# Retention attention, a capacity-routed mixture of experts and a gated MLP on one core: expert outputs stored from ScalarE's queue, five staging buffers, and new numbers in the planner

## The chip, the core and the metric

The kernel runs on one core of a Trainium2 chip. The metric is device time in microseconds for one execution; runs of an unchanged kernel here lay between 903.23 and 906.43 us. Everything is float32 outside; most products are made of three float32r matmuls (high part by high part, low by high, high by low).

## The reference

```python
# 1: retention attention, q, k, v: (4, 8, 576, 64)
scores = (q @ k.T) / sqrt(64);  out = (scores * decay(gamma_h, i - j, causal)) @ v
x = out.transpose(0, 2, 1, 3).reshape(2304, 512)
# 2: 8 experts, each token to one expert, cap = 288 tokens each
logits = x @ w_gate
for idx in argsort(-logits.flatten()):        # greedy, best logit first
    tok, e = idx // 8, idx % 8
    if assigned[tok] < 0 and counts[e] < cap: assigned[tok] = e; counts[e] += 1
for e in range(8): out[assigned == e] = relu(x[assigned == e] @ w1[e]) @ w2[e]   # 512 -> 1024 -> 512
# 3: 512 -> 2048 -> 512
h = x @ w_in;  return (h * tanh(softplus(h))) @ w_out
```

## The kernel before

There are three stages. **Attention** walks over 18 tiles of 128 tokens, computes the gate's logits and stores x in DRAM. **Experts**: the greedy assignment is rebuilt as a search. In each of 8 rounds the expert that fills first is found by VectorE (DVE) and TensorE (PE) in turn: six threshold steps, each a comparison `G` on DVE, 18 small matmuls `pF`, a test `sat`, one matmul `pD`. The round then gives the expert's number `eid`, the marks of its tokens, and through `pI` the list `idx` of its 288 tokens. GpSimd (POOL) gathers these rows of x into `xg` by three indirect DMAs; PE transposes them (`mmx`), ScalarE (ACT) rounds them to `xh`, DVE makes the rest `xl`. The expert's weights come in 8 units of 512 KB: SyncE (SP) reads `eid` into a register (line 532) and issues each load into a staging buffer `st` (3 of them); ACT rounds it to `whi` (line 562), POOL, late in the stage DVE too, makes `wlo` (line 565), after which the staging buffer is free. `whi` and `wlo` lie in a ring of 12. Per expert PE runs 96 matmuls `mma` (first layer; after every 12, ACT makes `hh` and DVE `hl`, which frees the PSUM bank) and 96 `mmb` (second layer, four outputs `y`). ACT copies each `y` out of PSUM (line 787) and SP stores it to `y_scratch` (line 650). There are 32 such stores of 144 KB.

In between, the weights of stage 3, which arrive as float64, are narrowed to float32 in 32 pieces: SP loads `std`, ACT makes `words`, DVE shifts (line 725) and joins into `dw` (line 728), ACT makes `dt`, POOL multiplies, SP stores `dw` to DRAM. **The last stage** reads y in 6 tiles of 384 tokens and the narrowed weights in 16 units (the same `st`, `whi`, `wlo`), and alternates per step 12 matmuls `mmc` and 9 matmuls `po`, with a gate of ACT, DVE and POOL operations between them.

From the experts on, the order on every engine is fixed when the program is built, by a planner inside the kernel. Every piece of work is a Python generator that yields the engine, an estimated duration, the events that it waits for and a priority; the planner keeps a clock per engine and emits the instruction that could start first. Each engine then runs its list strictly in order, SP's list of DMA issues too: an instruction whose input is late holds back everything behind it on that engine. An estimate that is short of the truth so puts an instruction too early in its list.

Of the kernel before, what the change touches and what calls it, by code (L numbers as in the profile page):

```python
# [7 lines left out]
F32 = mybir.dt.float32  # L8
# [9 lines left out]
P = 128  # L18
# [15 lines left out]
REST = 64.0  # L34
NRING = 12
YB = 4
# [7 lines left out]
GATHER = 7500  # L44
# [86 lines left out]
class Kernel:  # L131
# [188 lines left out]
    def routing_setup(self):  # L320
# [5 lines left out]
        self.onef = pr.tile([P, NT], F32, name="onef")  # L326
        nc.gpsimd.memset(self.onef, 1.0)
        self.digit = pr.tile([64, 6, P], BF16, name="digit")
# [45 lines left out]
    def route(self):  # L374
# [8 lines left out]
        for i in range(E):  # L383
# [4 lines left out]
            if i == E - 1:  # L388
# [3 lines left out]
                self.spawn(self.weights_of(junk, at))  # L392
                rest = rw.tile([P, NT], F32, name="rest")
                v.tensor_scalar(rest, self.dead, -1.0, 1.0, op0=ALU.mult, op1=ALU.add)
                v.tensor_tensor_scan(scan[:, 0], self.onef, rest, 0.0, op0=ALU.mult, op1=ALU.add)
# [14 lines left out]
            for s in range(6):  # L410
                m = WIDTHS[s]
                if s or i:
# [34 lines left out]
                    at = yield PE, 80 + 15 * m, [at], 0  # L447
# [8 lines left out]
            at = yield DVE, 2100, [at], 0  # L456
# [11 lines left out]
            over = self.at("over").rearrange("p (j t) -> p j t", j=2)  # L468
            v.tensor_tensor(over[:, 0], key, theta.to_broadcast([P, NT]), op=ALU.is_gt)
            v.tensor_tensor(over[:, 1], key, theta.to_broadcast([P, NT]), op=ALU.is_equal)  # L470
            of = over
# [14 lines left out]
            if i:  # L486
                self.widen(i, ohe)
                self.spawn(self.weights_of(junk, at))
                choice = yield from self.choose(i, at)
            at = yield DVE, 1600, [marked, at], 0  # L490
            pose = rw.tile([P, NT], F32, name="pose")
            v.scalar_tensor_tensor(pose, scan[:, 1], pP[:, 1:2], eq, op0=ALU.add, op1=ALU.mult)
            v.scalar_tensor_tensor(pos, scan[:, 0], pP[:, 0:1], gt, op0=ALU.add, op1=ALU.mult)
            fin = self.at("fin")
            v.scalar_tensor_tensor(fin, pose, CAP + 0.5, eq, op0=ALU.is_lt, op1=ALU.mult)
            if i == 0:
                self.spawn(self.weights_of(junk, at))
            v.tensor_tensor(self.dead, self.dead, gt, op=ALU.add)
            v.tensor_tensor(self.dead, self.dead, fin, op=ALU.add)
            v.tensor_tensor(pose, pose, fin, op=ALU.mult)  # L500
            v.tensor_tensor(pos, pos, pose, op=ALU.add)
# [19 lines left out]
    def weights_of(self, junk, at):  # L521
# [9 lines left out]
        at = yield SP, 1000, [at], 0  # L531
# [116 lines left out]
    def store(self, dst, src, at, done=None):  # L648
        at = yield SP, DMA_ISSUE, [at], 1
        self.nc.sync.dma_start(dst, src)  # L650
        if done is not None:
            done.append(self.arrival(100000, at))
# [10 lines left out]
    def y_place(self):  # L663

        n = self.made - YB
        return Event(0) if n < 0 else self.stored[n] if n < len(self.stored) else None

# [34 lines left out]
    def narrow(self):  # L702
# [4 lines left out]
        def at(k, n):  # L707
            return [lambda: done[k].get(n)] if n >= 0 else []

        def load():  # L710
            for n in range(32):
# [3 lines left out]
                now = yield SP, DMA_ISSUE, [Event(0), *at("read", n - 3)], self.narrow_priority  # L715
# [4 lines left out]
        def piece(n, st, now, dst):  # L720
# [5 lines left out]
            now = yield DVE, 680, [now, *at("store", n - 3)], self.narrow_priority  # L726
            out = self.conv.tile([P, 512], U32, name="dw", bufs=3)
# [10 lines left out]
            now = yield SP, DMA_ISSUE, [now], self.narrow_priority  # L738
# [27 lines left out]
    def experts(self):  # L766
        nc, a = self.nc, self.a
        for i in range(E):
# [14 lines left out]
            def result(i, d, bank, at):  # L783
                at = yield ACT, 410, [at, self.y_place], 0
# [295 lines left out]
```

## Time and profile before

| | |
|---|---|
| median of 3 runs | 904.78 us (903.23 to 906.43) |
| profiled execution, its own time | 900.87 us |
| its span, first to last instruction | 899.1 us |
| busy: PE, DVE, POOL, ACT | 810.1, 682.9, 484.0, 407.8 us |
| mean granted TensorE clock | 0.937 of full speed |

The profile comes from one execution, which was 0.4% quicker than the median; sums on its rows belong beside 900.87. Shares of the whole span hide that the stages have different limits, so the rows further down are cut by stage: attention to about 100 us, the first routing to 144, experts from 144 to about 460, the last stage from there.

### The profile page before, as it was taken

What the parts mean: (1) busy time and instruction counts of PE and PEld (TensorE: products, weight loads), DVE (VectorE), ACT (ScalarE), POOL (GpSimd) and SP (SyncE); (2) the same over time, 40 slices, a digit from 0 to 9 for tenths busy, and PEclk for the clock granted to TensorE, in tenths of its full rate; (3) what the DMA queues carried; (4) which work ended last, traced back from release to release, by engine and by line L of the source; (5) the groups of instructions that cost most, each with busy time, mean ns of one, the idle gap of its engine ahead of it and who ended that gap; (6) DMA issues with size and microseconds to landing.
All of it is one profiled execution on the core that took longest, in us unless ns stands there. A gap on an engine that the chain in (4) does not pass through costs nothing.

```text
span 899.1 us, 15492 instructions
## 1 busy us (share of the span) xinstructions
PE 810.1 (90%) x5833; PEld 726.6 (81%) x5833; DVE 682.9 (76%) x1104; ACT 407.8 (45%) x736; POOL 484.0 (54%) x406
## 2 busy tenths in 40 slices
PE   7999767969796979776999899997999999999997
PEld 5888636868786969676998789986899899999995
DVE  4344574748584768583778999998899899899894
ACT  1221214434443444434666655544655645645543
POOL 4533015756564566553424776755755655655644
PEclk9999888969897879896999999998999999999999
DMA  9982146777777777779976300200100100100000
GB/s 341 357 268 76 71 87 221 198 149 194 188 200 182 197 174 207 186 161 266 336 240 200 117 19 1 71 1 1 53 19 1 59 13 1 62 10 0 36 1 36
DMA packets 66331, 112.37 MB, mean 125 GB/s; under 512 B 10192, under 2 KB 38224, under 8 KB 66256
## 3 DMA queue, kind: packets, MB, share of 16 engines
q1 hardware_dynamic: 63280, 101.94, 39.8%
q0 software_dynamic: 2976, 9.44, 3.5%
q8 instruction: 46, 0.75, 0.4%
q14 instruction: 29, 0.24, 0.1%
HBM read 88.81 MB, written 22.55 MB: 124 GB/s over the span
## 4 chain that ended last, share of the span: by engine, by line
PE 54%; DVE 20%; DMA 18%; POOL 3%; issue 2%; ACT 1%; SPq 1%; POOLq 0%; DVEq 0%; ACTq 0%
PE mmc L959 15%; PE po L1020 15%; PE mma L753 9%; DVE q L989 8%; DMA st<-w 7%; DMA xg<-x_scratch,idx 5%; PE mmb L753 4%; DVE n L984 3%; DMA std<-w_in 3%; PE pA L200 2%; PE pT L228 2%; PE pT L231 2%; PE pL L241 2%; PE pF L450 1%; DVE n L994 1%
## 5 line engine op out<-in xcount | busy, mean ns | idle before, releaser
L989 DVE RECIPROCAL q<-q 128x384 f32<-128x384 f32 x96 | 244.3, 2545 | 10.6 <-ACT q L987 9.1
L565 POOL TENSOR_TENSOR wlo<-st,whi 128x1024 fp32r<-128x1024 f32 x53 | 125.8, 2384 | 99.3 <-ACT whi L562 92.7
L991 POOL TENSOR_TENSOR n<-n,q 128x384 f32<-128x384 f32 x96 | 102.0, 1062 | 99.3 <-DVE q L989 94.9
L1001 POOL TENSOR_TENSOR gl<-n,gh 128x384 fp32r<-128x384 f32 x96 | 109.0, 1135 | 55.6 <-ACT gh L999 55.3
L959 PE MATMUL mmc<-yh,whi 128*128 128x384 f32 x384 | 130.8, 341 | 8.0 <-DVE n L994 7.9
L959 PE MATMUL mmc<-yl,whi 128*128 128x384 f32 x384 | 130.5, 340 | 5.0 <-POOL yl L919 4.7
L959 PE MATMUL mmc<-yh,wlo 128*128 128x384 f32 x384 | 130.3, 339 | 0.0
L562 ACT CAST whi<-st 128x1024 fp32r<-128x1024 f32 x80 | 83.4, 1047 | 83.2 <-DMA st<-w 79.0
L1020 PE MATMUL po<-whi,gl 128*128 128x512 f32 x288 | 114.6, 398 | 0.0
L1020 PE MATMUL po<-wlo,gh 128*128 128x512 f32 x288 | 114.4, 397 | 0.0
L1020 PE MATMUL po<-whi,gh 128*128 128x512 f32 x288 | 112.8, 392 | 0.0
L984 DVE SCALAR_TENSOR_TENSOR n<-s 128x384 f32<-128x384 f32 x96 | 104.1, 1086 | 3.2 <-ACT s L977 2.5
L977 ACT ACTIVATE s<-mmc 128x384 f32<-128x384 f32 x96 | 47.1, 491 | 117.4 <-PE mmc L959 105.0
L753 PE MATMUL mma<-xh,whi 128*128 128x288 f32 x256 | 84.4, 330 | 6.8 <-ACT xh L624 4.4
L959 PEld LDWEIGHTS mmc<-yh,whi 128*128 128x128 f32 x384 | 72.7, 189 | 14.9 <-DVE n L994 9.1
L753 PE MATMUL mma<-xh,wlo 128*128 128x288 f32 x256 | 83.4, 326 | 0.0
L753 PE MATMUL mma<-xl,whi 128*128 128x288 f32 x256 | 83.1, 325 | 0.0
L959 PEld LDWEIGHTS mmc<-yl,whi 128*128 128x128 f32 x384 | 72.8, 189 | 10.1 <-POOL yl L919 5.3
L753 PE MATMUL mmb<-hl,whi 128*128 128x288 f32 x256 | 78.4, 306 | 0.0
L753 PE MATMUL mmb<-hh,wlo 128*128 128x288 f32 x256 | 77.7, 304 | 0.0
L753 PE MATMUL mmb<-hh,whi 128*128 128x288 f32 x256 | 77.7, 304 | 0.0
L736 POOL TENSOR_TENSOR dw<-dw,dt 128x512 f32<-128x512 f32 x32 | 48.5, 1516 | 48.0 <-ACT dt L732 45.3
(149 smaller groups left out, 1643.6 us busy)
## 6 DMA issues: line engine op xcount, KB each, us to landing
st<-w SPq DMA_DIRECT2D x64, 512.0 KB, 6.1
qk<-qk SPq DMA_DIRECT2D x18, 512.0 KB, 4.8
kv<-kv SPq DMA_DIRECT2D x18, 512.0 KB, 5.2
std<-w_in SPq DMA_DIRECT2D x16, 512.0 KB, 8.2
std<-w_out SPq DMA_DIRECT2D x16, 512.0 KB, 5.7
x_scratch<-xs SPq DMA_DIRECT2D x18, 256.0 KB, 2.8
y_scratch<-y SPq DMA_DIRECT2D x32, 144.0 KB, 6.0
yt<-y_scratch SPq DMA_DIRECT2D x22, 192.0 KB, 2.7
```

Source lines behind the costliest of these rows:

```text
L200: nc.tensor.matmul(pA[i][:, hp, :], QK[t][sl, 1, hp, :], QK[t][sl, 0, hp, :], start=True, stop=True)
L562: self.nc.scalar.copy(dst[0], st)
L565: (self.nc.vector if lo.engine == DVE else self.nc.gpsimd).tensor_tensor(dst[1], st, dst[0].bitcast(F32), op=ALU.subtract)
L736: nc.gpsimd.tensor_tensor(out, out, t, op=ALU.mult)
L753: self.nc.tensor.matmul(bank[1][:, :CAP], al if h == 2 else ah, bl if h == 1 else bh, start=(first and j == h == 0), stop=(last and j == n ...
L959: self.nc.tensor.matmul(bank[1][:, :TILE], (wl if h == 2 else wh)[:, c, cs], x[c][h == 1], start=(c == h == 0), stop=(c == HP - 1 and h == 2))
L977: nc.scalar.activation(s, p, AF.Sigmoid)
L984: v.scalar_tensor_tensor(u, s, 2.0, s, op0=ALU.subtract, op1=ALU.mult)
L989: v.reciprocal(q, q)
L991: nc.gpsimd.tensor_tensor(u, u, q, op=ALU.mult)
L1001: nc.gpsimd.tensor_tensor(gl, u, gh.bitcast(F32), op=ALU.subtract)
L1020: nc.tensor.matmul(po[j], (gl if h == 2 else gh)[:, js], (wl if h == 1 else wh)[:, f % 2], start=(f == h == 0), stop=(f == DFF // P - 1 an ...
```

## The change

- `result` no longer hands y to SP: ACT issues the store itself, directly behind its own copy. The planner counts the store as done 6,000 ns later (`STORED`).
- Staging buffers: `STAGES = 5` in place of 3. `dw` has 2 buffers in place of 3.
- Estimates: a gather takes 10,000 ns in place of 7,500, a product's matmul 150 in place of 132, `pF` 90 + 17m in place of 80 + 15m, the copy of y 480 in place of 410, two DVE stretches of the routing less.
- SP's instructions are planned 4,000 ns behind what they wait for (`APART`): the list store, the store of `dw`, the reload of `std`, the read of `eid` from the second expert on.
- Routing on DVE: the choice of tokens above and at the threshold takes one mask and two fused operations in place of two comparisons and two fused operations; one running sum over 36 columns replaces two over 18; after it, `dead` is updated once from `pos` in place of twice. Per round 13 operations become 10.

```diff
+STORED = 6000
+APART = 4000
+STAGES = 5
...
-GATHER = 7500
+GATHER = 10000
...
-            for j in range(2):
-                v.scalar_tensor_tensor(of[:, j], top, best[:, 0:1], over[:, j], op0=ALU.is_equal, op1=ALU.mult)
...
-            for j in range(2):
-                v.tensor_tensor_scan(scan[:, j], self.onef, of[:, j], 0.0, op0=ALU.mult, op1=ALU.add)
+            chosen = rw.tile([P, NT], F32, name="chosen")
+            v.tensor_scalar(chosen, top, best[:, 0:1], None, op0=ALU.is_equal)
+            v.scalar_tensor_tensor(gt, key, theta[:, 0:1], chosen, op0=ALU.is_gt, op1=ALU.mult)
+            v.scalar_tensor_tensor(eq, key, theta[:, 0:1], chosen, op0=ALU.is_equal, op1=ALU.mult)
+            v.tensor_tensor_scan(scan.rearrange("p j t -> p (j t)"), self.onef, self.at("over"), 0.0, op0=ALU.mult, op1=ALU.add)
...
-            v.tensor_tensor(self.dead, self.dead, gt, op=ALU.add)
-            v.tensor_tensor(self.dead, self.dead, fin, op=ALU.add)
...
+            v.scalar_tensor_tensor(self.dead, pos, 0.5, self.dead, op0=ALU.is_gt, op1=ALU.add)
...
-        at = yield SP, 1000, [at], 0
+        at = yield SP, 1000, [at if i == 0 else Event(at.t + APART)], 0
...
-        place = [lambda: self.staged.get(n - 3)] if n >= 3 else []
+        place = [lambda: self.staged.get(n - STAGES)] if n >= STAGES else []
...
-            now = yield DVE, 680, [now, *at("store", n - 3)], self.narrow_priority
-            out = self.conv.tile([P, 512], U32, name="dw", bufs=3)
+            now = yield DVE, 680, [now, *at("store", n - 2)], self.narrow_priority
+            out = self.conv.tile([P, 512], U32, name="dw", bufs=2)
...
-            now = yield SP, DMA_ISSUE, [now], self.narrow_priority
+            now = yield SP, DMA_ISSUE, [Event(now.t + APART)], self.narrow_priority
...
-                at = yield PE, 132, [lambda: (term() or (0, None))[1], *([] if bank else [self.bank])], 2
+                at = yield PE, 150, [lambda: (term() or (0, None))[1], *([] if bank else [self.bank])], 2
...
-                at = yield ACT, 410, [at, self.y_place], 0
+                at = yield ACT, 480, [at, self.y_place], 0
...
-                yield from self.store(a["y"][:, d, i * CAP:(i + 1) * CAP], y, at, self.stored)
+                nc.scalar.dma_start(a["y"][:, d, i * CAP:(i + 1) * CAP], y)
+                self.stored.append(Event(at.t + STORED))
...
-        self.stage = ctx.enter_context(tc.tile_pool(name="stage", bufs=3))
+        self.stage = ctx.enter_context(tc.tile_pool(name="stage", bufs=STAGES))
```

With these numbers the planner writes another list for every engine. Three places follow.

The first place is SP's queue where it loads the third expert's weights, before: `w1` and `w2` are that expert's weights, `y` the outputs of the second, `w_in` and `w_out` pieces to be narrowed, an `ISA` the address of the next load.

```order
L548 DMA st_2758<-w2 128x2x512
L717 DMA std_2770<-w_in 128x1024
L650 DMA y_scratch<-y_2765 128x288
L650 DMA y_scratch<-y_2791 128x288
L650 DMA list_scratch<-idx_2725 96x3x1
L739 DMA w_out32<-dw_2728 128x512
L650 DMA y_scratch<-y_2854 128x288
L717 DMA std_2874<-w_out 128x1024
L548 ISA
L548 DMA st_2904<-w2 128x2x512
L739 DMA w_in32<-dw_2845 128x512
L650 DMA y_scratch<-y_2928 128x288
```

Now, the same expert's loads:

```order
L549 DMA st_2624<-w1 128x4x256
L549 ISA
L549 DMA st_2630<-w1 128x4x256
L549 ISA
L549 DMA st_2635<-w1 128x4x256
L549 ISA
L549 DMA st_2641<-w1 128x4x256
L549 ISA
L549 DMA st_2651<-w2 128x2x512
L549 ISA
L549 DMA st_2750<-w2 128x2x512
L720 DMA std_2812<-w_out 128x1024
```

The four stores of y between the fifth and the eighth load are gone from SP's queue, and six loads stand in a row where five did.

The second place is ACT, the second expert's first layer (`hh` from `mma10`, `mma11`, ...), before:

```order
L562 CAST whi_2366<-st_2287 128x1024
L732 ACTIVATE dt_2400<-std_1749 128x512
L776 ACTIVATE hh_2415<-mma10_2361 128x288
L723 ACTIVATE words_1379<-std_2157 128x512
L562 CAST whi_2434<-st_2341 128x1024
L776 ACTIVATE hh_2448<-mma11_2408 128x288
L562 CAST whi_2475<-st_2373 128x1024
L776 ACTIVATE hh_2492<-mma12_2441 128x288
L776 ACTIVATE hh_2524<-mma13_2487 128x288
L776 ACTIVATE hh_2542<-mma14_2521 128x288
```

Now:

```order
L790 COPY y_2351<-mmb03_2169 128x288
L792 DMA y_scratch<-y_2351 128x288
L563 CAST whi_2354<-st_2276 128x1024
L625 CAST xh_2131<-mmx1_2358 128x288
L625 CAST xh_2131<-mmx1_2366 128x288
L625 CAST xh_2131<-mmx1_2371 128x288
L625 CAST xh_2131<-mmx1_2376 128x288
L563 CAST whi_2412<-st_2332 128x1024
L779 ACTIVATE hh_2438<-mma10_2404 128x288
L779 ACTIVATE hh_2476<-mma11_2430 128x288
L779 ACTIVATE hh_2515<-mma12_2478 128x288
L779 ACTIVATE hh_2544<-mma13_2512 128x288
```

The casts of weights that stood between the `hh` have moved ahead of them, and the store of y is a DMA of ACT's own list.

The third place is PE, the transposes `mmx5` of the sixth expert's gathered rows, before (the `pF` ahead of them is the 18th of a routing step):

```order
L450 MATMUL pF_4851<-oh_4490,G_4839 31x8
L634 MATMUL mmx5_4871<-cst_65,xg_4664 128x96 x3
L634 MATMUL mmx5_4882<-cst_65,xg_4664 128x96 x3
L634 MATMUL mmx5_4887<-cst_65,xg_4664 128x96 x3
L634 MATMUL mmx5_4892<-cst_65,xg_4664 128x96 x3
L455 LDWEIGHTS digit_116
L455 MATMUL pD_4897<-sat_4876,digit_116 128x8
L753 MATMUL mma50_4902<-xh_4668,whi_4557 128x288
```

Now:

```order
L756 MATMUL mmb40_4642<-hl_4646,whi_4325 128x288
L635 MATMUL mmx5_4804<-cst_65,xg_4551 128x96 x3
L635 MATMUL mmx5_4815<-cst_65,xg_4551 128x96 x3
L635 MATMUL mmx5_4820<-cst_65,xg_4551 128x96 x3
L459 LDWEIGHTS digit_117
L459 MATMUL pD_4825<-sat_4808,digit_117 128x8
L756 MATMUL mmb40_4642<-hh_4625,wlo_4326 128x288
L756 MATMUL mmb40_4642<-hh_4650,whi_4325 128x288
L756 MATMUL mmb40_4642<-hl_4679,whi_4325 128x288
L756 MATMUL mmb40_4642<-hh_4650,wlo_4326 128x288
L756 MATMUL mmb41_4643<-hh_4625,whi_4325 128x288
```

Before, all of the fifth expert's matmuls stand ahead of the transposes and `mma50` follows them; now 58 of its `mmb` stand behind the first transposes and ahead of `mma50`. Counted from the last `pI` of an expert (its token list) to its first `mmx`, the second, third, fifth and seventh expert have 64, 77, 78 and 88 large matmuls where 49, 59, 44 and 59 stood.

## Rows read from the trace of the kernel before

**Rows 1.** Windows by stage: length; busy PE, PEld, DVE, ACT, POOL; clock; DMA; GB/s.

```profile
144.00:460.00 316.00, 267.91 (x2305) 251.14 (x2305) 210.85 (x599) 139.66 (x244) 177.31 (x100) 0.88 0.78 203
460.00:614.00 154.00, 140.97 (x721) 126.32 (x720) 145.65 (x112) 87.69 (x162) 96.53 (x80) 0.98 0.25 80
614.00:878.00 264.00, 264.00 (x1312) 238.85 (x1313) 247.02 (x189) 146.13 (x275) 155.12 (x161) 0.99 0.07 22
```

**Rows 2.** Waits of PE from 140 to 460 us: total, times, longest.

```profile
PE mmx L634 <- DMA xg<-x_scratch,idx: 22.4, 6, 7.2
PE pF L450 <- DVE G L432: 12.7, 2, 7.1
PE mma L753 <- ACT xh L624: 4.4, 1, 4.4
PE mma L753 <- DVE xl L626: 2.4, 1, 2.4
```

**Rows 3.** Timeline of PE: start, us, instruction, idle before it and its releaser.

```profile
187.55 1.86 PE L634 MATMUL mmx<-cst,xg 96*128 96x96 f32 x10 [7.22 <-DMA xg<-x_scratch,idx]
...
230.22 1.86 PE L634 MATMUL mmx<-cst,xg 96*128 96x96 f32 x10 [3.06 <-DMA xg<-x_scratch,idx]
...
285.93 0.64 PE L450 MATMUL pF<-oh,G 128*32 128x8 bf16 x18 [7.08 <-DVE G L432]
...
321.79 1.86 PE L634 MATMUL mmx<-cst,xg 96*128 96x96 f32 x10 [1.76 <-DMA xg<-x_scratch,idx]
...
405.73 1.86 PE L634 MATMUL mmx<-cst,xg 96*128 96x96 f32 x10 [5.23 <-DMA xg<-x_scratch,idx]
```

**Rows 4.** Chain that ended last, 225 to 241 us: start, us, what.

```profile
225.57 0.41 ACT y L787
...
226.00 0.33 SPq L650
...
226.58 11.77 DMA st<-w
...
238.37 1.05 ACT whi L562
239.42 0.32 ACT hh L776
...
240.14 0.15 DVE sat L371
```

**Rows 5.** The same chain: two gathers, and 96 matmuls in a row.

```profile
172.39 15.12 DMA xg<-x_scratch,idx
...
307.71 14.03 DMA xg<-x_scratch,idx
...
432.74 12.79 PE mmb L753 x96
```

**Rows 6.** Waits of SP's queue from 100 to 460 us.

```profile
SPq L650 <- ACT y L787: 43.7, 25, 6.4
SPq L548 <- POOL wlo L565: 30.3, 14, 4.3
```

**Rows 7.** DMA issues: count, KB each, median us to landing.

```profile
st<-w SPq DMA_DIRECT2D x64, 512.0 KB, 6.1
...
y_scratch<-y SPq DMA_DIRECT2D x32, 144.0 KB, 6.0
...
w_out<-dw SPq DMA_DIRECT2D x16, 256.0 KB, 7.5
```

**Rows 8.** Waits of ACT and DVE from 100 to 460 us.

```profile
ACT whi L562 <- DMA st<-w: 79.0, 34, 10.0
...
DVE dw L728 <- DMA w_out<-dw: 4.2, 2, 2.6
```

**Rows 9.** Groups of DVE from 140 to 395 us: busy, mean ns, idle before.

```profile
L476 DVE TENSOR_TENSOR_SCAN scan<-onef,sc 128x18 bf16<-128x18 f32 x12 | 1.7, 180 | 0.2
...
L469 DVE TENSOR_TENSOR sc<-sc,theta 128x18 f32<-128x18 f32 x6 | 1.1, 185 | 0.2
```

More of the change, by code (lines that the diff above doesn't have):

```diff
@@ L391, in route @@
                 v.tensor_tensor(junk, self.open, rc[:, RC["eid"]], op=ALU.mult)
-                self.spawn(self.weights_of(junk, at))
+                self.spawn(self.weights_of(junk, at, i))
                 rest = rw.tile([P, NT], F32, name="rest")
                 v.tensor_scalar(rest, self.dead, -1.0, 1.0, op0=ALU.mult, op1=ALU.add)
-                v.tensor_tensor_scan(scan[:, 0], self.onef, rest, 0.0, op0=ALU.mult, op1=ALU.add)
+                v.tensor_tensor_scan(scan[:, 0], self.onef[:, :NT], rest, 0.0, op0=ALU.mult, op1=ALU.add)
                 at = yield PE, 30, [at], 0
@@ L455, in route @@
                 nc.tensor.matmul(pD, self.digit[:m, s, :], sat[:m], start=True, stop=True)
-            at = yield DVE, 2100, [at], 0
+            at = yield DVE, 1700, [at], 0
             most = rw.tile([P, 1], F32, name="most")
@@ L467, in route @@
             v.tensor_reduce(best, full, AX.X, ALU.max)
[L468 to L471, printed above, removed]
[L472 to L476 removed]
+            of = self.at("over").rearrange("p (j t) -> p j t", j=2)
+            gt, eq = of[:, 0], of[:, 1]
+            chosen = rw.tile([P, NT], F32, name="chosen")
[3 more added lines that the diff above has]
+            v.tensor_tensor_scan(scan.rearrange("p j t -> p (j t)"), self.onef, self.at("over"), 0.0, op0=ALU.mult, op1=ALU.add)
             marked = yield PE, 190, [at], 0
@@ L487, in route @@
                 self.widen(i, ohe)
-                self.spawn(self.weights_of(junk, at))
+                self.spawn(self.weights_of(junk, at, i))
                 choice = yield from self.choose(i, at)
-            at = yield DVE, 1600, [marked, at], 0
-            pose = rw.tile([P, NT], F32, name="pose")
+            at = yield DVE, 1350, [marked, at], 0
+            pose = self.at("fin")
             v.scalar_tensor_tensor(pose, scan[:, 1], pP[:, 1:2], eq, op0=ALU.add, op1=ALU.mult)
             v.scalar_tensor_tensor(pos, scan[:, 0], pP[:, 0:1], gt, op0=ALU.add, op1=ALU.mult)
-            fin = self.at("fin")
-            v.scalar_tensor_tensor(fin, pose, CAP + 0.5, eq, op0=ALU.is_lt, op1=ALU.mult)
+            fin = rw.tile([P, NT], F32, name="short")
+            v.tensor_scalar(fin, pose, CAP + 0.5, None, op0=ALU.is_lt)
             if i == 0:
-                self.spawn(self.weights_of(junk, at))
-            v.tensor_tensor(self.dead, self.dead, gt, op=ALU.add)
-            v.tensor_tensor(self.dead, self.dead, fin, op=ALU.add)
-            v.tensor_tensor(pose, pose, fin, op=ALU.mult)
-            v.tensor_tensor(pos, pos, pose, op=ALU.add)
+                self.spawn(self.weights_of(junk, at, i))
+            v.tensor_tensor(fin, pose, fin, op=ALU.mult)
+            v.tensor_tensor(pos, pos, fin, op=ALU.add)
+            v.scalar_tensor_tensor(self.dead, pos, 0.5, self.dead, op0=ALU.is_gt, op1=ALU.add)
             self.spawn(self.tokens(i, pos, at))
@@ L646, in arrival, with store @@
         return Event(self.time["dma"] + DMA_WAIT)
-    def store(self, dst, src, at, done=None):
-        at = yield SP, DMA_ISSUE, [at], 1
+    def store(self, dst, src, at):
+        at = yield SP, DMA_ISSUE, [Event(at.t + APART)], 1
         self.nc.sync.dma_start(dst, src)
-        if done is not None:
-            done.append(self.arrival(100000, at))
     def bank(self):
@@ L666, in y_place, with apart @@
         return Event(0) if n < 0 else self.stored[n] if n < len(self.stored) else None
+    def apart(self, e):
+        return e and Event(e.t + APART)
     def take_bank(self, name):
@@ L714, in load @@
                 r = slice(r * P, r * P + P)
-                now = yield SP, DMA_ISSUE, [Event(0), *at("read", n - 3)], self.narrow_priority
+                now = yield SP, DMA_ISSUE, [Event(0), *[lambda: self.apart(e()) for e in at("read", n - 3)]], self.narrow_priority
                 st = self.conv.tile([P, 512, 2], U32, name="std", bufs=3)
```

7 lines of the change are left out of this document (4 added, 3 removed).

## The prediction

> **What bounds the kernel now.** I read the windows by stage first, since shares of the whole span mix three limits. From 614 to 878 us PE is busy in every microsecond at full clock [rows 1]; the change takes no matmul away there, so this stretch stays as it is. From 460 to 614 PE misses 13 us of 154. The expert stage, 144 to 460, is another case: PE works 267.9 of 316 us, is idle for 48.1, and the granted clock is 0.88 [rows 1], a mix of the two levels 1.2 and 2.4 GHz. No other engine is full there (DVE 211, POOL 177, ACT 140 of 316), and DMA is busy 0.78. So the stage is bound by waits in lists that run in order. Everything that can be won is there, at most the 48.1 us of idle PE and what the low clock takes.
>
> The waits of PE say who ends the idle time: the gathered rows 22.4 us, `G` from DVE 12.7 us, `xh` 4.4 us and `xl` 2.4 us [rows 2]. The timeline gives the single ones: 7.22, 3.06, 1.76 and 5.23 us in front of transposes, 7.08 us in front of a `pF` [rows 3]. The chain of waits shows what is behind the last kind [rows 4]: ACT copies a y at 225.57, SP issues its store at 226.00, and only then the load behind it in SP's list, at 226.58. Its weights are landed 11.77 us later; ACT, which stands at that load's `whi` in its list, casts at 238.37, does `hh` behind it, and DVE gets to `sat`, for which PE waits. A store that nobody needs soon holds a load, the load holds ACT, and ACT holds PE. Summed up, SP's queue waits 43.7 us for copies of y and 30.3 us for a staging buffer to be freed [rows 6], and ACT 79.0 us for weights [rows 8].
>
> **The change part by part.** The sum is made against the profiled execution's own 900.87 us; the median of the runs is 904.78, 3.9 us more, which I add at the end.
>
> *Transposes later.* The chain has 15.12 and 14.03 us of gather in it, from issue to landing [rows 5], where the planner reckoned with 7.5 us; so it put the transposes too early and PE stood. Now it reckons with 10 us and with 150 ns per matmul. A large matmul takes 12.79 / 96 = 0.133 us [rows 5]. Between token list and transposes the second expert has 15 matmuls more (64 for 49), the third 18, the fifth 34, the seventh 29: 2.0, 2.4, 4.5 and 3.9 us of work that covers the wait. Of 7.22, 3.06, 1.76 and 5.23 us [rows 3] that takes 2.0, 2.4, 1.76 and 3.9, together 10.1 us. The remaining 5.1 of the 22.4 us belong to the first expert, which has nothing to run meanwhile. Ends: 0, if gathers become slower by as much, and 17.3.
>
> *Loads earlier, casts out of the way.* With y off SP's list and five buffers, five loads can leave at once, and the order on ACT puts most casts ahead of the `hh`. The waits that ACT's casts cause are the 12.7 us for `G` and the 6.8 us for `xh` and `xl` [rows 2], 19.5 us. In the later experts casts still stand between `hh`, so I take half, 9.8 us, between 0 and 19.5.
>
> *Clock.* The mean of 0.88 over 316 us lacks 0.12 x 316 = 38 us of full speed [rows 1]. If the idle 48.1 us all ran at the lower level they would make up 24, so about 14 us are lost on a PE that works. I give back the share of idle time that goes, 19.9 / 48.1 = 0.41: 5.8 us; ends 0 and 14.
>
> *Routing on DVE.* Three operations fewer per round, of some 0.18 us each [rows 9], less what the sum over 36 columns takes more than one over 18 (at most 0.18 us): 0.36 to 0.54 us, for seven rounds 2.5 to 3.8. DVE has 105 us to spare in the stage, so half of 3.1 lies on the path: 1.6 us, between 0 and 3.8.
>
> *The stores on ACT.* The trace has no DMA issued by ACT. SP takes 0.33 us to issue the same store [rows 4]; ACT may be as quick, or cost as much as its whole copy, 0.41 us, if it has to wait for that to be written. I take 0.4 us, with 0 and 0.8 as ends: 32 x 0.4 = 12.8 us. ACT is free for 176 of 316 us [rows 1], but what is queued behind a store (`words`, `whi`, `xh`) is waited for now and then; a third on the path is 4 us lost; ends 0 and 13. SP's own 32 x 0.33 us come off a queue that has time, worth nothing by themselves. If the copy of y is late itself, the next `hh` is what comes late behind it, as it was before.
>
> *Two `dw` buffers.* A piece's DVE step now waits for the store two pieces back, and such stores take 7.5 us to land [rows 7]. With three buffers it waited only twice, 4.2 us in all [rows 8]. The planner spaces pieces for it, so I take 2 us; ends 0 and 22 (of 32 such waits of 2.1 us, 67 us, half would lie beside free DVE and a third of the rest beside free PE).
>
> *Last stage.* Its weights are staged further ahead; the 13 us that PE misses between 460 and 614 come mostly from the gate's DVE work, which is the same. I take 0, between a loss of 3 and a gain of 5.
>
> Sum: 10.1 + 9.8 + 5.8 + 1.6 - 4 - 2 = 21.3 us. 900.87 - 21.3 = 879.6; with the 3.9 us, **883.5 us**.
>
> **A rule against the change.** By the Trainium skill, "DMA: Bandwidth & Descriptors", section "Issuing engines are not separate DMA queues", transfers started by ScalarE, SyncE or GpSimd run on the same 16 DMA engines, and starting them on several engines saves only the sequencer's time to start them. Its words are of transfer time; the row on SP's 43.7 us of waiting [rows 6] is about which instructions stand behind which, of which it says nothing. By the rule alone the stores' move would bring nothing and cost ACT's issue.
>
> **The rivals.** *The stores' move brings nothing.* The five buffers are freed by POOL's `wlo`, for which SP waits 30.3 us anyway [rows 6]; where that is the later of the two waits, the y store in front was no loss. For it: in the row of 226.58 one late buffer follows one late store. Against it: 43.7 us in 25 waits is more. Then the term on loads falls to 4 us and the clock's to 4.1: 883.5 + 5.8 + 1.7 = 891 us.
>
> *Gathers get slower.* Two more staging buffers let 1.05 MB more of weights be in flight when a gather starts. At 203 GB/s with a DMA share of 0.78, 260 GB/s when busy [rows 1], that is 4.0 us; for six gathers 24 us, which all lands on PE if the transposes stand where the older gather would have ended. This cancels the sum: 903 to 907 us. It decides from 3.5 us per gather (21.3 / 6). Against it: weights loaded in a burst early are not in flight later, when the gather runs.
>
> *Slower: `dw` with two buffers.* If the step at `dw` holds DVE for a piece's whole landing time instead of an occasional 2.1 us, `hl`, `xl` and `sat` stand behind it, and PSUM banks and routing with them. From 21.3 / 32 = 0.7 us per piece on the path the gain is gone; at 1.0 us it is 883.5 + 32 = 915 us. For it: 7.5 us of landing [rows 7] against two buffers. Against it: only 4 pieces fall on one expert.
>
> *Nearly all waits go.* With 17.3, 19.5 and 14 us in the three large terms: 50.8 + 1.6 - 6 = 46 us, 858 us. Against it: seven rounds of routing remain a chain of DVE and PE steps.
>
> **How the numbers follow.** A 0.3% step, 2.7 us, is about what a measurement can tell here. My forecast, 872 to 889, has 0.43; the stores' move worth nothing 0.18, all faster; slower gathers 0.15 (0.06 faster, 0.06 the same, 0.03 slower); `dw` and other new waits 0.14 (0.12 slower, 0.02 the same); nearly all waits gone 0.10. Faster is 0.43 + 0.18 + 0.06 + 0.10 = 0.77, the same 0.08, slower 0.15. The range from 860 to 908 leaves out the far end of the best case and most of the `dw` case, about 0.18.
>
> **What the changed profile would show.** If right: an expert stage of some 295 us with a clock above 0.90; waits of PE for gathered rows near 12 us in place of 22.4 and hardly a wait for `G` above 3 us; ACT waiting clearly less than 79 us for weights; SP's queue without waits for y; loads of weights in bursts of five; the last stage as it was. The stores on ACT should show some 0.4 us each. Wrong would be: gathers of 17 us and more with waits before the transposes as before (slower gathers); long waits of DVE at line 731 for stores of `dw` (two buffers); waits of PE for `xh` or of `hh` behind copies of y (ACT's list); SP waiting for `wlo` as long as it now waits for y (nothing moved).

## The result and the profile after

The changed kernel takes **887.99 us** (median of 4 runs, 883.57 to 892.24) where the kernel before takes 904.0 (4 runs beside it, 896.34 to 906.43): ratio 0.986, 95% interval 0.981 to 0.990. The medians are 16.0 us apart, 1.8%; the ratio, of fast runs alone, is smaller, 1.4%. Forecast were 883.5 and a range of 860 to 908. The profiled execution took 883.97 us, 16.9 less than that of before; the sum of the prediction had 21.3. The sum came out near, but most of its terms did not, and that they made up for one another was luck. The prediction took 2.7 us for what a measurement can tell; over all runs here the unchanged kernel took 888.2 to 906.6 us, so a few us between two kernels of four runs each are not told apart.

Windows of the changed kernel, as in [rows 1], with the first routing ahead of them:

```profile
100.00:144.00 44.00, 34.57 (x321) 21.44 (x323) 30.62 (x108) 13.09 (x19) 15.41 (x8) 0.71 0.62 172
144.00:460.00 316.00, 266.74 (x2296) 250.04 (x2292) 212.66 (x576) 146.74 (x250) 177.96 (x100) 0.90 0.78 215
460.00:614.00 154.00, 148.44 (x746) 135.07 (x747) 143.16 (x115) 85.75 (x165) 94.45 (x85) 0.97 0.13 44
614.00:870.00 256.00, 256.00 (x1294) 232.42 (x1293) 244.76 (x186) 143.29 (x270) 155.20 (x161) 1.00 0.07 22
```

Between 144 and 460 us PE is idle for 316 - 266.7 = 49.3 us; before it was 48.1 [rows 1]. So the idle time has not gone, the clock alone has risen, from 0.88 to 0.90 (a second profile of the changed kernel has 48.1 us idle and 0.89, so most of this is within the spread). Where PE works more is ahead of 144 us (34.6 us; the same window of before had 28.0) and from 460 to 614 (148.4 for 141.0 in [rows 1]). From 614 on PE is full in both. What PE waits for has changed, though (as in [rows 2], 140 to 460 us):

```profile
PE pD L459 <- DVE sat L375: 16.4, 6, 4.7
PE pF L454 <- DVE G L436: 8.0, 2, 7.8
PE mmx L635 <- DVE xl L627: 6.2, 1, 6.2
PE mma L756 <- ACT xh L625: 5.8, 1, 5.8
PE pF L454 <- DVE known L441: 4.7, 2, 4.4
PE mmb L756 <- DVE xl L627: 3.4, 1, 3.4
```

Waits for gathered rows, 22.4 us in [rows 2], are gone to nothing. In their place stand waits for DVE: `sat` 16.4 us, `G` 8.0, `xl` 9.6 in two rows. For `sat` PE had waited little before:

```profile
PE pD L455 <- DVE sat L371: 3.6, 6, 1.4
```

Why DVE is late, its own waits tell, with those of ACT and SP's queue (100 to 460 us, as in [rows 6, 8]):

```profile
ACT whi L563 <- DMA st<-w: 44.3, 22, 7.1
...
DVE dw L731 <- DMA w_in<-dw: 24.7, 5, 9.7
```

```profile
SPq L720 <- DVE dw L731: 60.9, 14, 15.4
SPq L549 <- POOL wlo L566: 60.2, 19, 8.8
```

ACT waits for weights 44.3 us in place of 79.0, as hoped. But DVE waits 24.7 us for stores of `dw` to `w_in` to land (and 1.9 for those to `w_out`), where it waited 4.2 [rows 8]; and SP waits 60.2 us for staging buffers where `wlo` held it 30.3 and y 43.7 [rows 6]. One such wait of DVE, 256 to 275 us. SP's queue, the chain, DVE and PE, in this order:

```profile
256.23 0.40 SPq L720 DMA_DIRECT2D std<-w_out  x1
256.67 0.42 SPq L652 DMA_DIRECT2D list_scratch<-idx  x1
257.15 0.59 SPq L742 DMA_DIRECT2D w_in<-dw  x1
```

```profile
257.15 15.44 DMA w_in<-dw
...
272.70 0.75 DVE dw L731
...
273.79 0.74 DVE G L436
```

```profile
272.70 0.75 DVE L731 SCALAR_TENSOR_TENSOR dw<-std,ic,words 128x512 uint32<-128x512 uint32 x1 [9.73 <-DMA w_in<-dw]
```

```profile
266.49 0.29 PE L756 MATMUL mmb<-hh,whi 128*128 128x288 f32 x1
274.59 0.65 PE L454 MATMUL pF<-oh,G 128*31 128x8 bf16 x18 [7.81 <-DVE G L436]
...
277.18 0.44 PE L756 MATMUL mmb<-hl,whi 128*128 128x288 f32 x1
```

The 256 KB store of 257.15 lands 15.44 us later. The piece two behind needs its buffer, so DVE stops for 9.73 us at line 731, in the middle of a routing step whose `sc`, `Tu` and `G` stand right behind; PE runs out of matmuls at 266.8 and waits until 274.59. A large matmul that started every 0.13 us before that wait starts every 0.24 behind it: the lower of the two levels of the clock (granted clock 0.50 from 274.6 to 277.2 us).

What the store stands behind on SP's queue are six loads of weights started from 240.4 us on, one of `std`, and directly ahead of it the store of a token list, 288 elements of 4 bytes. What DMA moved from 255 to 274 us, in 40 slices of 0.475 us (busy tenths, then GB/s):

```profile
DMA  0000369999999904002434979889999929319999
GB/s 0 0 0 30 56 237 379 448 392 384 260 295 331 72 22 17 0 0 2 11 20 13 68 74 89 61 133 70 42 87 58 33 9 74 15 39 262 386 428 440
```

Nothing moves in the first three slices, so the loads issued before 255 us had landed; the last load ahead of the list (255.74) and the `std` behind it are done at 261.2 us, in the 14th slice. For the 4 us behind it nearly nothing moves, at most 22 GB/s, then 9 to 133 until 272. The load issued behind the store, at 258.07, is done at 273.9 only. The DMA engines are not idle then. From 265 to 272 us they are busy for 0.98 of the time, at 57 GB/s (last two numbers):

```profile
265.00:272.00 7.00, 1.78 (x14) 1.54 (x12) 0.00 (x0) 0.00 (x0) 0.00 (x0) 0.80 0.98 57
```

A row of the page of before that the prediction passed over tells how long such a list takes to land (KB each, median us):

```profile
list_scratch<-idx SPq DMA_DIRECT2D x8, 1.1 KB, 14.5
```

1.1 KB take 14.5 us, where 512 KB of weights take 6.1 [rows 7]. All stores of `dw` on the chain of waits that took 10 us and more (10.5, 15.4, 10.8, 15.7) are the first to follow a list on SP's queue; the three others took 5.4, 4.3 and 7.2.

The place on SP's queue is not what counts, though. ACT's own stores of y, on another queue, are as late:

```profile
257.79 0.33 ACTq L792 DMA_DIRECT2D y_scratch<-y  x1
259.15 0.33 ACTq L792 DMA_DIRECT2D y_scratch<-y  x1
```

They took 15.1 and 15.0 us. (Such a time runs from the issue to the last of the events by which the trace counts a transfer as done.) Between 120 and 470 us, the eight stores of y that ACT issued while a list was on its way took 8.7 to 15.1 us, median 11.1, and 20 others 1.7 to 6.9, median 3.2; for `dw` it is nine with a median of 12.4 against 23 with 4.2. The kernel before has the same split, 12 stores of `dw` with a median of 13.9 against 20 with 5.6: its median of 7.5 [rows 7] hides two kinds. The medians are split like this in every trace here, but no kernel leaves the list out, so whether the list makes the others late or is late with them stays open.

Where the 16.9 us show. The last stage computes 96 reciprocals `q`. The first starts at 469.5 us (before 472.8), the 48th at 666.4 (681.5), the last at 865.5 (882.4): 3.3 us were gained when it begins, 15.0 after half of it. What lies in between are casts of weights not done yet. Groups from 460 to 614 us, before and after:

```profile
L989 DVE RECIPROCAL q<-q 128x384 f32<-128x384 f32 x32 | 81.3, 2540 | 0.5 <-ACT q L987 0.5
...
L565 DVE TENSOR_TENSOR wlo<-st,whi 128x1024 fp32r<-128x1024 f32 x14 | 19.5, 1408 | 3.7 <-ACT whi L562 3.6
L562 ACT CAST whi<-st 128x1024 fp32r<-128x1024 f32 x17 | 17.8, 1045 | 4.1 <-DMA st<-w_out 2.1 <-DMA st<-w_in 1.9
```

```profile
L993 DVE RECIPROCAL q<-q 128x384 f32<-128x384 f32 x35 | 88.9, 2541 | 2.5 <-ACT q L991 2.5
...
L563 ACT CAST whi<-st 128x1024 fp32r<-128x1024 f32 x7 | 7.2, 1044 | 3.1 <-PE mmb L756 2.7 <-ACT y L790 0.4
L566 DVE TENSOR_TENSOR wlo<-st,whi 128x1024 fp32r<-128x1024 f32 x5 | 6.7, 1346 | 3.2 <-ACT whi L563 3.2
```

DVE is the full engine from 500 us on (40.0 of the 40 us to 540 before). Before, it still had 14 `wlo` of weights to make there, 19.5 us; now 5, 6.7 us. The 12.8 us are three more `q` tiles in the same time (35 for 32). The expert stage ended no earlier, the last copy of y stands at 475.9 us (before 475.2); it left less behind.

### The profile page after: what moved, and what is told of

It reads as the page before. It is cut to its first block, busy times and chain, and to the rows that moved or that the text cites. A ratio compares the mean times of both kernels' runs of the same rounds, so it can differ in the third digit from the quotient of the medians.

```text
span 882.2 us, 15451 instructions
## 1 busy us (share of the span) xinstructions
PE 805.3 (91%) x5833; PEld 724.1 (82%) x5836; DVE 674.4 (76%) x1080; ACT 409.2 (46%) x736; POOL 484.3 (55%) x410
## 4 chain that ended last, share of the span: by engine, by line
PE 46%; DVE 21%; DMA 16%; issue 6%; POOL 5%; ACT 2%; SPq 2%; POOLq 0%; DVEq 0%; ACTq 0%
PE mmc L963 14%; PE po L1024 13%; DVE q L993 8%; DMA w_in<-dw 7%; PE mma L756 4%; DMA st<-w 4%; DVE n L988 4%; PE mmb L756 4%; PE pA L203 2%; PE pL L244 2%; PE pT L231 2%; PE pT L234 2%; POOL wlo L566 2%; DMA std<-w_in 2%; DVE n L998 2%
## 5 line engine op out<-in xcount | busy, mean ns | idle before, releaser
L995 POOL TENSOR_TENSOR n<-n,q 128x384 f32<-128x384 f32 x96 | 99.1, 1032 | 114.9 <-DVE q L993 107.7
L566 POOL TENSOR_TENSOR wlo<-st,whi 128x1024 fp32r<-128x1024 f32 x56 | 135.1, 2431 | 39.7 <-ACT whi L563 38.5
L563 ACT CAST whi<-st 128x1024 fp32r<-128x1024 f32 x80 | 82.3, 1046 | 63.3 <-DMA st<-w 44.3
L756 PE MATMUL mmb<-hh,whi 128*128 128x288 f32 x256 | 83.3, 326 | 4.9 <-DVE xl L627 3.4
L756 PE MATMUL mma<-xh,whi 128*128 128x288 f32 x256 | 80.6, 315 | 5.8 <-ACT xh L625 5.8
L756 PE MATMUL mmb<-hh,wlo 128*128 128x288 f32 x256 | 82.8, 323 | 0.0
L756 PE MATMUL mmb<-hl,whi 128*128 128x288 f32 x256 | 82.8, 323 | 0.0
L739 POOL TENSOR_TENSOR dw<-dw,dt 128x512 f32<-128x512 f32 x32 | 42.6, 1333 | 71.8 <-DVE dw L731 22.7
L756 PE MATMUL mma<-xh,wlo 128*128 128x288 f32 x256 | 79.1, 309 | 0.0
L756 PE MATMUL mma<-xl,whi 128*128 128x288 f32 x256 | 78.4, 306 | 0.0
```

The costliest lines, as they stand in the source:

```text
L563: self.nc.scalar.copy(dst[0], st)
L566: (self.nc.vector if lo.engine == DVE else self.nc.gpsimd).tensor_tensor(dst[1], st, dst[0].bitcast(F32), op=ALU.subtract)
L739: nc.gpsimd.tensor_tensor(out, out, t, op=ALU.mult)
L756: self.nc.tensor.matmul(bank[1][:, :CAP], al if h == 2 else ah, bl if h == 1 else bh, start=(first and j == h == 0), stop=(last and j == n ...
L995: nc.gpsimd.tensor_tensor(u, u, q, op=ALU.mult)
```

## The experiments

Ratios are to the kernel before on the same chip, with 95% intervals. The changed kernel again and kernels 1, 4 and 6 ran on one chip, 2, 3, 5 and 7 on a second, 8 to 11 on a third, so differences of medians across these groups are rough. "New" estimates are those of the change; kernels 9 and 10 exchange three of them.

| kernel | staging | `dw` | y from | estimates | median us | ratio |
|---|---|---|---|---|---|---|
| changed, again | 5 | 2 | ACT | new | 884.1 | 0.988 (0.978 to 0.998) |
| 1 | 4 | 3 | ACT | new | 867.0 | 0.968 (0.958 to 0.978) |
| 2 | 4 | 2 | ACT | new | 883.5 | 0.989 (0.978 to 0.999) |
| 3 (before, two `dw`) | 3 | 2 | SP | old | 912.8 | 1.021 (1.012 to 1.029) |
| 4 `dw` stored by POOL | 5 | 2 | ACT | new | 915.4 | 1.021 (1.009 to 1.033) |
| 5 | 3 | 3 | ACT | new | 872.8 | 0.976 (0.968 to 0.984) |
| 6 | 5 | 2 | SP | new | 885.7 | 0.986 (0.975 to 0.998) |
| 7 (before, y from ACT) | 3 | 3 | ACT | old | 898.2 | 1.001 (0.997 to 1.006) |
| 8 | 4 | 3 | SP | new | 865.2 | 0.964 (0.959 to 0.969) |
| 9 (before, new estimates) | 3 | 3 | SP | new | 885.8 | 0.985 (0.979 to 0.991) |
| 10 | 4 | 3 | ACT | old | 890.7 | 0.992 (0.989 to 0.996) |
| 11 (before, new routing) | 3 | 3 | SP | old | 899.7 | 1.000 (0.997 to 1.003) |

The theory after the result: two `dw` buffers cost far more than the 2 us forecast (what makes the stores late was at first taken to be the bursts of loads). The rivals: the stores of y, the staging depth, or the estimates explain the time, and the waits at `dw` lie beside free time. Each edit makes the planner write all lists anew, so none changes one thing and leaves the order of the rest.

**The changed kernel again.**

> The changed kernel once more, as the measure for the runs beside it on the same chip. Expected by every theory: 0.986 of the kernel before, 884 to 892 us, with waits of DVE at line 731 for stores of `dw` of some 25 us in all between 100 and 460 us.

884.1 us, ratio 0.988, as expected.

**1 and 2. Three `dw` buffers.** A fifth staging buffer and a third of `dw` don't fit together, so the first kernel takes four and three, and the second then takes the third `dw` buffer away again.

```diff
-STAGES = 5
+STAGES = 4
...
-            now = yield DVE, 680, [now, *at("store", n - 2)], self.narrow_priority
-            out = self.conv.tile([P, 512], U32, name="dw", bufs=2)
+            now = yield DVE, 680, [now, *at("store", n - 3)], self.narrow_priority
+            out = self.conv.tile([P, 512], U32, name="dw", bufs=3)
```

> The changed kernel with three `dw` buffers (as before the change) and four staging buffers in place of five, all else as changed. Theory (two `dw` buffers cost about 8 us on the path): DVE's waits at line 731 under 8 us, time 880 to 884 us, if the fifth staging buffer is worth 2 us or less. Rival (staging buffers are what brings the gain): 891 to 897 us, with ACT's waits for weights well over 44 us.

867.0 us, a larger gain than expected. The second kernel has the edit of `STAGES` alone:

> The changed kernel with four staging buffers in place of five; `dw` keeps two. Theory (the third `dw` buffer brought the 17 us by which the kernel with three `dw` and four staging buffers beat the changed one): 883 to 892 us, ratio to the kernel before about 0.986, DVE's waits at line 731 for stores 15 us or more between 100 and 460 us. Rival (the fifth staging buffer is what costs, since bursts of five loads stand ahead of the other transfers): 865 to 872 us, ratio 0.965 to 0.972.

883.5 us: the theory's side. The fifth staging buffer neither brings nor costs anything that can be told; the third `dw` buffer alone is worth 16.6 us by the medians, 2.1 points by the ratios. DVE's waits for these stores, 100 to 460 us, with three buffers and with two:

```profile
DVE dw L731 <- DMA w_in<-dw: 9.4, 2, 8.3
...
DVE dw L731 <- DMA w_out<-dw: 3.0, 2, 2.6
```

```profile
DVE dw L731 <- DMA w_in<-dw: 38.7, 6, 10.0
...
DVE dw L731 <- DMA w_out<-dw: 7.2, 2, 6.6
```

12.4 us against 45.9. The stores are no quicker with three (nine of them issued while a list was on its way, median 13.9 us); DVE only needs them later. With three, no wait of PE for `G` is left and 11.1 us for `sat`; with two they are 8.1 and 19.8. The window from 144 to 460 us with three shows what the prediction had looked for there:

```profile
144.00:460.00 316.00, 285.19 (x2413) 266.98 (x2413) 225.79 (x595) 162.17 (x278) 181.35 (x104) 0.94 0.83 232
```

PE is idle for 30.8 us, the clock is at 0.94, and the first `q` starts at 444.7 us.

**3. Two `dw` buffers in the kernel before.**

```diff
-            now = yield DVE, 680, [now, *at("store", n - 3)], self.narrow_priority
-            out = self.conv.tile([P, 512], U32, name="dw", bufs=3)
+            now = yield DVE, 680, [now, *at("store", n - 2)], self.narrow_priority
+            out = self.conv.tile([P, 512], U32, name="dw", bufs=2)
```

> The kernel before, with two `dw` buffers in place of three and nothing else. Theory (two `dw` buffers cost about 17 us, whatever the rest): 910 to 920 us, ratio 1.012 to 1.022, DVE's waits for stores of `dw` 15 us or more where before had 4.2. Rival (two `dw` buffers cost only together with five loads at once in SP's ring): within 4 us of the kernel before.

912.8 us, ratio 1.021: as the theory has it, with three staging buffers and y on SP too. So the loss doesn't need five loads at once.

```profile
DVE dw L728 <- DMA w_out<-dw: 29.3, 6, 9.0
...
DVE dw L728 <- DMA w_in<-dw: 12.8, 3, 9.5
```

42.1 us where three buffers had 4.2 [rows 8]. Here too the first store behind a list is the long one, six times on the chain of waits, 12.8 to 15.0 us; the three others there took 5.5 to 6.6. Over the whole stage, twelve stores of `dw` issued while a list was on its way took 12.0 to 15.0 us, 17 others 3.2 to 6.6. The list itself stands on it once, and the `dw` directly behind it:

```profile
400.83 11.16 DMA list_scratch<-idx
...
412.05 14.56 DMA w_out<-dw
```

**4. `dw` stored from POOL's queue.**

```diff
-            now = yield POOL, 1310, [now, sign], self.narrow_priority
+            now = yield POOL, 2300, [now, sign], self.narrow_priority
...
-            now = yield SP, DMA_ISSUE, [Event(now.t + APART)], self.narrow_priority
-            nc.sync.dma_start(dst, out)
+            nc.gpsimd.dma_start(dst, out)
```

> The changed kernel, but each store of `dw` is issued by POOL right behind POOL's own multiplication instead of by SP behind loads of weights. Theory (256 KB stores stand behind bursts of loads in SP's ring, land 10.5 to 15.7 us after issue, and with two buffers hold DVE and the routing behind it): landing of these stores falls under 9 us, DVE's waits at line 731 from 25 us to under 8, PE's waits for `sat` from 16 us to under 9, and the time by 5 to 10 us, 878 to 883 us. Rival (these waits lie where DVE has time, the transposes or the routing chain are what counts): within 2 us of the changed kernel. Other side: POOL's issue of 32 stores delays `wlo` and `yl`; then SP waits longer for staging buffers and the time rises by 3 us or more.

915.4 us: far on the other side. The way named there shows, SP waits longer for staging buffers (58.8 us in the changed kernel beside it):

```profile
SPq L549 <- POOL wlo L566: 80.1, 19, 9.3
```

But DVE's waits for stores at line 731 only fell from 28.0 to 17.4 us, and a new wait came up that nothing had named, of PE for the running sum `scan`, 28.5 us. DVE and POOL at one of them:

```profile
234.47 9.17 DVE L475 TENSOR_SCALAR chosen<-top,best 128x18 f32<-128x18 f32 x1
243.67 0.24 DVE L476 SCALAR_TENSOR_TENSOR sc<-sc,theta,chosen 128x18 f32<-128x18 f32 x1
```

```profile
233.73 0.58 POOL L741 DMA_DIRECT2D w_out<-dw  x1 [0.30 <-POOL dw L739]
234.34 9.27 POOL L566 TENSOR_TENSOR wlo<-st,whi 128x1024 fp32r<-128x1024 f32 x4
```

`chosen`, 18 columns wide, takes 0.24 us when POOL is free; here 9.17, and it ends within 0.03 us of the end of four `wlo` on POOL. Four times that makes 9.17 + 9.36 + 8.73 + 1.93 - 4 x 0.24 = 28.2 us, as much as PE's new wait. On what holds `dw` the run says that leaving SP's queue does not free it: issued by POOL, eleven stores took 6.3 to 11.8 us (median 10.4) while a list was on its way, 19 others 2.3 to 8.7 (median 4.0). And it found a cost of the routing's new form that the planner doesn't know.

**5. The buffers of before, the rest of the change.** Kernel 1 with

```diff
-STAGES = 4
+STAGES = 3
```

> The changed kernel with the buffers of before: three for staging, three for `dw`; what stays of the change is the y stores on ACT, the routing's fewer operations and the planner's estimates. Theory (three `dw` buffers are worth 17 us, staging buffers beyond three a few): 866 to 878 us. Rival 1 (deeper staging is the source of the gain, as the prediction's term on loads has it): 885 to 895 us, with ACT's waits for weights near the 79 us of before. Rival 2 (the fifth buffer alone costs): as with four staging buffers and two `dw`, whatever that gives.

872.8 us, within the theory's 866 to 878. Deeper staging is not where the gain comes from: four in place of three bring 5.8 us by the medians, and the intervals of kernels 1 and 5 overlap. ACT waits 49.8 us for `st<-w` with three buffers, 38.0 with four.

**6 to 8. The stores of y.** In kernels 6 and 8 (where the planner, unlike before, places each store 4,000 ns behind its copy):

```diff
-                nc.scalar.dma_start(a["y"][:, d, i * CAP:(i + 1) * CAP], y)
-                self.stored.append(Event(at.t + STORED))
+                yield from self.store(a["y"][:, d, i * CAP:(i + 1) * CAP], y, at)
+                self.stored.append(Event(at.t + APART + STORED))
```

> The changed kernel, but the stores of y go back to SP's list; five staging buffers, two `dw` buffers and the new estimates stay. Theory (the stores' move is a part of the gain, since a store waiting for its copy holds loads behind it): ACT waits for weights rise from 44 us towards 60, and the time is 4 to 8 us over the changed kernel's, 892 to 896 us. Rival 1 (the move brings nothing, the fifth buffer and the estimates bring it): within 2 us of the changed kernel. Rival 2 (the move costs: ACT held 9.1 us behind one store, 0.33 us for each of 32): 3 to 6 us less than the changed kernel, 882 to 885 us.

885.7 us against 884.1 beside it: rival 1. SP waits 23.9 us for copies of y again, ACT 58.0 for weights, and the time is the same as far as four runs from 878.9 to 891.5 us tell. The other way round, the kernel before with

```diff
-                yield from self.store(a["y"][:, d, i * CAP:(i + 1) * CAP], y, at, self.stored)
+                nc.scalar.dma_start(a["y"][:, d, i * CAP:(i + 1) * CAP], y)
+                self.stored.append(Event(at.t + 6000))
```

> The kernel before, with the stores of y issued by ACT and nothing else (three staging buffers, three `dw`). The prediction's terms (stores off SP's list help loads, less ACT's issue): some 5 us faster, 893 to 898 us. Rival (the stores' move brings nothing, as the changed kernel with y back on SP lets one think): within 3 us of the kernel before, and SP waits as long for staging buffers as it did for y and these together.

Ratio 1.001: nothing. SP waits 43.4 us for `wlo` now, where `wlo` held it 30.3 us and y 43.7 [rows 6]: part of the wait moved, the rest was not on the path. And in the fastest kernel, y back on SP:

> The fastest kernel so far (three `dw` buffers, four for staging), with y's stores back on SP. Theory (the stores' move brings nothing): within 3 us of that kernel's 867, so 862 to 871 us. Rival (with `dw` out of the way the stores on SP's list hold loads again, as the prediction's term on loads has it): 872 us or more, with SP waiting 20 us or more for copies of y and ACT more than 45 us for weights.

865.2 us against 867.0: nothing a third time, although SP waits 20.1 us for y there and ACT 50.7 for weights. Of the three, kernel 7 with its interval of half a percent is the one that excludes the 4 to 8 us of the theory.

**9 and 10. The planner's estimates.** Kernel 9 is the kernel before with

```diff
-GATHER = 7500
+GATHER = 10000
...
-                    at = yield PE, 80 + 15 * m, [at], 0
+                    at = yield PE, 90 + 17 * m, [at], 0
...
-                at = yield PE, 132, [lambda: (term() or (0, None))[1], *([] if bank else [self.bank])], 2
+                at = yield PE, 150, [lambda: (term() or (0, None))[1], *([] if bank else [self.bank])], 2
```

> The kernel before with the planner's new estimates alone: a gather at 10 us, a large matmul at 150 ns, a counting matmul at 90 + 17 m ns. The prediction's term (transposes later, 10.1 us, with the clock's share of it, 3 us): 885 to 890 us, and PE's waits for gathered rows near 12 us or less in place of 22.4. Theory after the runs so far (the changed kernel with three buffers of both kinds is 27 us faster than before, the stores' move and the deeper staging are worth little, so nearly all of it must be here or in the routing): 878 to 885 us. Rival (the gain is the routing's, which sets when the token lists are made): within 4 us of the kernel before.

885.8 us: the prediction's term. No instruction of the kernel is added or removed, only the order differs, and the wait for gathered rows (140 to 480 us) falls from 22.4 us to

```profile
PE mmx L634 <- DMA xg<-x_scratch,idx: 8.3, 5, 3.2
```

Part of what these waits give back returns as others: `sat` 10.8 us for 3.6, and PE's idle time from 144 to 460 us falls from 48.1 to 44.8 us only. So the 13.4 us by which the ratio puts kernel 9 ahead are shown for the three numbers together; that covered gathers bring them is argued. The new 150 ns, at least, are not nearer to the 133 ns that [rows 5] show for a matmul than the old 132.

Kernel 10 takes the same numbers back in the fastest one:

> The fastest kernel so far (three `dw` buffers, four for staging) with the estimates of before: a gather at 7.5 us, a large matmul at 132 ns, a counting matmul at 80 + 15 m ns. Theory (the estimates bring most of the gain): 880 us or more, with 10 us or more of waits of PE for gathered rows. Rival (the gain is the routing's, the staging's and the spacing of SP's list): within 5 us of 867.

890.7 us, 23.7 over kernel 1, or 2.4 points by the ratios. The size is the theory's, its place is not: waits for gathered rows are 4.4 us, not 10; `G` is late by 8.9 and `scan` by 5.5 us. The estimates also order DVE against PE. And the gathers themselves are quicker where `APART` puts the list's store behind them: the third gather of the second to the seventh expert takes 3.8 to 6.0 us here and 3.0 to 9.4 in the changed kernel, but 8.3 to 15.1 in the kernel before and 9.1 to 14.0 in kernel 9 (the sixth expert's is missing there), where the list's store is issued among the gathers or right behind them.

**11. The routing's operations in the kernel before:** the lines of the change from `over` to `dead`, whose core is shown with the change, and

```diff
-            at = yield DVE, 2100, [at], 0
+            at = yield DVE, 1700, [at], 0
...
-            at = yield DVE, 1600, [marked, at], 0
+            at = yield DVE, 1350, [marked, at], 0
```

> The kernel before with the routing's DVE operations as changed (one scan in place of two, fewer comparisons) and their two shorter due times, nothing else. The prediction's term (three operations fewer in each of seven rounds, half of it on the path): 1.6 us, 896 to 900 us. Rival (seven rounds of DVE and PE steps are a chain that sets the stage, so more than the operations' own time comes back): 8 us or more faster, under 892 us.

899.7 us, ratio 1.000 (0.997 to 1.003): no gain that can be told.

## Why the prediction was nearly right, step by step

- *Transposes later (10.1 us):* right in size, and in mechanism only in part. By itself (9) it is 1.5%, 13.4 us, and the sum had 10.1 and a share of the clock; in the kernel with room for `dw` (10 to 1) it is 23.7. That waits for gathered rows went by all of 22.4 us, the first expert's share too, has a second reason that the sum lacks: the gathers land sooner, as said under 10, and kernel 10 with the old estimates has 4.4 us of these waits left. What that is worth in time, no run shows.
- *Loads earlier, casts out of the way (9.8):* did not come there. PE's waits for `G`, `xh` and `xl` were 19.5 us and are 8.0 + 5.8 + 9.6 = 23.4. With three `dw` buffers (1) they are 6.3 (`xh` 2.0, `xl` 4.3), though `sat` stands at 11.1 there; but in kernel 9, where neither loads nor buffers changed, they are 9.7 already, so it is not shown that earlier loads are what took them away. That y's stores on SP's list were the cause is refuted by 7, and 6 and 8 agree: a store that waits on the chain can be replaced by the next wait (a staging buffer) at no gain. The chain of [rows 4] leads to a `sat`, not to the wait of 7.08 us for `G` that it was read for. The chain of that one has no y in it:

```profile
268.90 2.24 POOL wlo L565
271.14 11.77 DMA st<-w
...
285.12 0.77 DVE G L432
...
285.93 0.64 PE pF L450 x18
```

The load waited for a staging buffer, and both loads, here and in [rows 4], took 11.77 us (median 6.1 [rows 7]) while a list was on its way.
- *Clock (5.8):* 0.02 x 316 = 6.3 us by the windows (half of that in the second profile, 0.89), though idle PE did not shrink between 144 and 460 us. If right in size, then not by its reason: luck.
- *Routing (1.6):* nothing measurable. The seven `chosen` of the changed kernel take 236 to 1216 ns, 3.97 us together, 2.3 more than at 236 each; that can eat most of the 2.5 to 3.8 us of work that the prediction had as saved.
- *Stores on ACT (-4):* 0.33 us each, as SP's. Three comparisons show no cost and no gain (7 to half a percent, 6 and 8 to about one). By the Trainium skill, "DMA: Bandwidth & Descriptors", section "Issuing engines are not separate DMA queues", the move saves the issuing sequencer's time alone; the ratio of 1.001 agrees.
- *Two `dw` buffers (-2):* **the term that failed.** The mechanism was named, and the rival "slower" was put at 0.7 us per piece as its point of decision. Measured are 16.6 us (2 against 1), 0.52 per piece, and 2.1% in the kernel before. I took 7.5 us of landing and the planner's spacing as enough. The median hid that the stores issued while a token list is on its way, nine of 32 here, take 9.6 to 15.7 us; three buffers cover that, two don't, and DVE works in order, so the routing stands behind `dw`. The sign that the prediction had named for this, long waits of DVE at line 731, is what the profile showed. That it does not take five loads at once is shown by kernel 3. The long landings go with the list in every trace and on every queue, but no run took the list away, so that it is the cause is argued.
- *Last stage (0):* wrong place. 13.6 of 16.9 us (16.9 less the 3.3 at its start) show there, not because its steps changed but because 9 `wlo` fewer remain for DVE, which is full there. The gain of the expert stage was read at its end, where it doesn't show; the count of casts left over shows it.

Of the rivals, "the stores' move brings nothing" holds as a mechanism, but 891 us was not its result, since its loss was made up elsewhere; "gathers get slower" went the other way, they land sooner; "nearly all waits go" is near what kernel 8 reaches, 865.2 us. From kernel to kernel: before to 9 by estimates -1.5%; 9 to 5 (routing, stores of y, the spacing `APART`) -0.9 points; 5 to 1 (fourth staging buffer) -0.8; 1 to 2 (`dw`) +2.1; 2 to the changed one 0. The step from 9 to 5 is not settled: routing and y are worth nothing alone, `APART`, with which the quicker gathers go, was not tried alone, and the intervals overlap. So the forecast came near by luck: `dw` cost some 15 us more than put down, and that was made up by the steps from 9 to 5 and from 5 to 1, together 1.7 points or some 15 us, for which the sum had 9.8 - 4 + 1.6 us and other reasons.

## What to carry to other kernels

A buffer saved from an in-order engine's output costs what stands behind that engine's wait, so price it with the longest landing that the trace shows, and look on all queues for what is on its way then, not with a median; here the third 256 KB `dw` buffer was worth 16.6 us and the fifth staging buffer nothing that could be told. A planner's estimates, of which the trace contradicted one (gather 7.5 against 14 to 15 us on the chain), are the cheapest thing to change: three of them together brought 1.5% without touching an instruction. A wait at the top of a list is worth only what the next wait on the same instruction leaves: move one thing alone and measure, before it goes into a change with five others.

## What the hardware showed unasked

A one-input `TENSOR_SCALAR` on DVE, 128x18 f32 to f32, waits while POOL runs `TENSOR_TENSOR`: 0.24 us when POOL is free, up to 9.36 in kernel 4 when four `wlo` follow one another there. By the Trainium skill, "SBUF — State Buffer", section "Who interferes with whom", such an operation can take the port pair that DVE shares with GpSimd, and the one that comes second blocks for the first one's whole instruction. The trace agrees that it blocks. In the changed kernel the wait ends with the POOL instruction that was running (four of seven `chosen`, 0.56 to 1.22 us, each to within 0.04 us of its end); in kernel 4 it lasted three times over a row of four of 2.4 us each, not one. Why there, is not shown.

A store on ACT's queue normally costs it 0.33 us, but in the changed kernel one was issued at 272.94 us, 9.1 us behind its copy (263.42 to 263.82), and the next `xh` with it:

```profile
263.42 0.40 ACT L790 COPY y<-mmb 128x288 f32<-128x288 f32 x1 [1.17 <-PE mmb L756]
272.94 0.33 ACTq L792 DMA_DIRECT2D y_scratch<-y  x1
273.30 1.31 ACT L625 CAST xh<-mmx 128x288 fp32r<-128x288 f32 x4 [9.48 <-DMA y_scratch<-y]
```

What it waited for was ACT's own store of y from 257.79, one of the two that took 15 us: at 272.88 us the trace has ACT's wait for the semaphore by which that store counts as done, whose last event is at 272.86, and the new store uses the same semaphore. So a late store held ACT's casts though nothing needed its data.
